# Two loads of attention input ahead of the last two quarters of a weight matrix: the order of transfers in a fused attention and expert kernel

## The chip, the cores and the metric

The kernel runs on one core of a Trainium2 chip. A core has five engines with their own instruction queues: PE (TensorE, matrix multiply), DVE (VectorE), ACT (ScalarE), POOL (GpSimd) and SP (SyncE, which here only issues DMAs). The metric is the device time of one execution in microseconds (us); a comparison uses the median of several.

## What is computed

Two stages follow each other. The first is causal linear attention with decay over 4 sequences of 768 positions with 8 heads of 64, in f32. The second takes the attention output as 3072 tokens of 512 values and applies a gated layer with `w_in` (512 x 2048) and `w_out` (2048 x 512).

```python
for b in range(nb):                      # blocks of 64 positions
    intra = einsum('bhic,bhjc->bhij', qb, kb) * Dmask
    intra = einsum('bhij,bhjd->bhid', intra, vb)
    inter = einsum('bhid,bhde->bhie', qb * lam_pow, kv_state)
    out[:, :, sl] = intra + inter
    kv_state = lam_block * kv_state + einsum('bhsd,bhse->bhde', kb * rev_pow, vb)
x = out.transpose(0, 2, 1, 3).reshape(3072, 512)
h = x @ w_in
result = (h * cos(h)) @ w_out
```

## The kernel before, in words

**Tiles.** The 3072 tokens are 24 blocks of 128 tokens, numbered n = 0 to 23. The second stage takes them in nine tiles of 4, 2, 2, 2, 2, 2, 2, 4 and 4 blocks (TILES). Blocks 0 to 3, tile 0, come from two "spans", the first 256 positions of two sequences, and have code of their own (add_span, L579). From block 4 on, blocks go in "ordinary pairs": pair 2 is blocks 4 and 5, pair 3 is blocks 6 and 7, and so on.

**What a tile does.** For each of 16 slices f of the hidden width, four matmuls make a slice of h in PSUM (ps_h, L732), ACT takes the cosine (L738), DVE multiplies (g, L744). Then each block is projected with w_out: 16 matmuls of 512 columns, in four groups of four (ps_f, L778), so that each group needs one quarter of w_out. ACT copies the result (L792), and SP stores it.

**What an ordinary pair does.** Loads of q, k and v (f32, 256 KB each, L253 through add_load, L275), a product or a cast to bf16 for each of the six (prepare, L315: q at L329, k at L333, v at L337), transposes of q and k (for pair 2 on PE, L359, with copies by DVE at L362; from pair 3 on by DMA, L365), scores (ps_s, L407) and masks (DVE, L412), values (ps_o, L470), the update of the carried state (ps_kv, L419), and the carried part (L502). For pair 2 the first q and the second v are prepared by DVE, the second q and the first v by POOL, and both k by ACT.

**The order of the work.** A planner (L57) holds a task list with a duration, an engine, dependencies and a due time for each task. It plays the list through and gives each engine a fixed order of instructions; nothing is reordered later. A DMA is two tasks: the issue on SP or POOL, and a transfer on one shared "DMA" engine. So a changed duration or dependency of one transfer can move any instruction of the program, on any engine.

**The order of the loads.** ORDER (L36) lists the first loads by name: q, k and v of the two spans (q0 to v1), the six pieces of w_in (i0 to i5), the four quarters of w_out (o0 to o3), and the first ordinary loads (q4, q5, k4, k5). After the list come v4 and v5 and all later pairs. The pieces of both weight matrices are cast to bf16 on the way and are issued by POOL (add_w, L294); a quarter of w_out is 512 KB in bf16. All other loads named here are issued by SP. The loop at L817 to L832 turns the list into tasks, and adds a few waits between SP's and POOL's queues by hand:

- q4 waits for nothing by its place, but `pace` (L755, L851, and the manual dependency at L284) makes it wait for DVE's product g of slice 13 of tile 0.
- o3 waits for the landing of q4 (L825).
- v4 waits for the landing of k4 (L823).

`start` (L252) turns such a wait into a semaphore wait of the issuing instruction, so that everything behind it on that queue waits too.

In the order that the planner gives to PE, tile 0's slices of h are followed by its 64 projection matmuls, among which lie the transposes, scores and values of pair 2. Fifty-six of the 64 stand ahead of pair 2's values (L470), and the first that needs o2 is the thirteenth at the earliest.

Of the kernel before, what the change touches and what calls it, by code (L numbers as in the profile page):

```python
# [18 lines left out]
SPANS = 2  # L19
# [6 lines left out]
LOAD_US = 1.22  # L26
# [6 lines left out]
OUTS = [{"qT": ("ACT", "ACT"), "kT": ("ACT", "ACT")}, {"qT": ("ACT", "ACT"), "kT": ("ACT", "ACT")}]  # L33
VALUES_OUT = [("ACT", "ACT"), ("DVE", "ACT")]
STATE_OUT = [("ACT", "ACT"), ("ACT", "ACT")]
ORDER = "q0 k0 q1 k1 v0 v1 i0 i1 i2 i3 i4 i5 o0 o1 o2 q4 q5 k4 k5 o3"  # L36

W_IN = [2, 2, 1, 3, 4, 4]

# [105 lines left out]
def kernel(  # L145
# [23 lines left out]
    def where(n):  # L169

        if n < 2 * SPANS:
            return n // 2, n % 2
        g, c = divmod(n // 2, NB)
        return 2 * g + n % 2, c
# [4 lines left out]
    loads = ctx.enter_context(tc.tile_pool(name="loads", bufs=BUFS["ld"]))  # L179
# [61 lines left out]
    load_t, issue_t = {}, {}  # L241
    last_issue = {}

    def dma(queue, us, issue_us, emit, prio, deps=(), get=None, ordered=True, lat=1.9):
        t = pl.add(queue, issue_us, list(deps) + [last_issue.get(queue) if ordered else None], emit, prio, get=get)
        if ordered:
            last_issue[queue] = t
        d = pl.add("DMA", us, [t], None, prio, lat=lat)
        d.issue = t
        return t, d  # L250

    def start(queue, o, x, deps):  # L252
        i = queue.dma_start(out=o, in_=x)  # L253
        for d in deps:
            tc.add_manual_dep(i.ins, d.issue.ins.ins.name, mybir.DependencyInfo(
                mybir.DependencyClass.Sync, mybir.DependencyReason.DATA), reason="order of loads")
        return i

    def add_span_load(name, src, x, prio, deps):
        def emit(_):  # L260
            if on_pool:
                t = span_v[x]
            else:
                if ("raw", x) not in live:
                    live["raw", x] = work.tile([P, 2, H, 2, D], F32, tag="g", name="sp_f")
                t = live[name, "sp", x] = live["raw", x][:, "qk".index(name[0])]
            return start(nc.gpsimd if on_pool else nc.sync, t.rearrange("u h s d -> u h (s d)"),
                         src[x, :, 0:2 * P, :].rearrange("h (u s) d -> u h (s d)", s=2), deps)

        on_pool = name == "v_f"  # L270
        issue, load_t[name, "sp", x] = dma("POOL" if on_pool else "SP", 1.5, 1.0 if on_pool else 0.5, emit, prio, deps,
                                           lat=0.95 if on_pool else 1.0)
        return load_t[name, "sp", x]

    def add_load(n, name, src, prio, deps=()):  # L275
        b, c = where(n)

        def emit(_):
            t = loads.tile([P, H, D], F32, tag=name, name=name)
            live[name, n] = t  # L280
            i = start(nc.sync, t, src[b, :, c * P:(c + 1) * P, :].transpose([1, 0, 2]), deps)
            if (name, n) == ("q_f", 2 * SPANS):

                tc.add_manual_dep(i.ins, pace[0].ins.ins.name, mybir.DependencyInfo(  # L284
                    mybir.DependencyClass.Sync, mybir.DependencyReason.DATA), reason="order of loads")
            return i

        issue_t[name, n], load_t[name, n] = dma("SP", LOAD_US, 0.85, emit, prio, deps, get=name,
                                                lat=1.9 if name == "v_f" and n < 2 * SPANS + 2 else 1.0)
        return load_t[name, n]  # L290

    w_t, pace = {}, []

    def add_w(which, c, prio, deps=()):  # L294
        def emit(_):
            if which == "in":
                a, z = sum(W_IN[:c]) * P, sum(W_IN[:c + 1]) * P
                return start(nc.gpsimd, w_in_sb[:, :, a:z], w_in_src[:, :, a:z], deps)
            a, z = c * KF // WCH, (c + 1) * KF // WCH
            return start(nc.gpsimd, w_out_sb[:, a:z, :], w_out_src[:, a:z, :], deps)  # L300

        part = W_IN[c] / 4 if which == "in" else 1.0
        early = which == "in" and c < 3
        _, w_t[which, c] = dma("POOL", 2.68 * part, 0.8, emit, -2000.0 if early else prio, deps,
                               lat=1.2)
        return w_t[which, c]
# [503 lines left out]

    names = ORDER.split()
    for pr in range(SPANS, NBLK // 2):
# [4 lines left out]
    for at, name in enumerate(names):  # L817
        which, n = name[0], int(name[1:])
        soft = which in "io"
        deps = [kept[-3 if soft else -2]] if at and (names[at - 1][0] in "io") != soft else []  # L820
        if name == f"q{2 * SPANS}":
            deps = []
        if name == f"v{2 * SPANS}":  # L823
            deps = [load_t["k_f", 2 * SPANS]]
        if name == "o3":  # L825
            deps = [load_t["q_f", 2 * SPANS]]
        if soft:
            kept.append(add_w({"i": "in", "o": "out"}[which], n, at, [] if at < 9 else deps))
        elif n < SPANS and at < 9:
            kept.append(add_span_load(which + "_f", src[which], n, at - 2040, kept[0:1] if name == "v0" else []))  # L830
        else:
            kept.append(add_load(n, which + "_f", src[which], at, deps))  # L832
# [15 lines left out]
        add_ffn(i)  # L848
    for f in range(3, SPLIT):
        hid[2 * f].deps.append(spans[1]["carried"])  # L850
    issue_t["q_f", 2 * SPANS].deps += pace  # L851
    closing.deps.append(v12[SPANS])
    first_sum.deps += Vo[2 * SPANS]
    lead_end = hid[2 * SPLIT]
# [76 lines left out]
```

## Time and profile before

| what | us |
|---|---|
| median of 3 runs | 202.83 (202.78 to 202.98) |
| profiled execution, its time | 202.54 |
| profiled execution, its span | 200.8 |
| PE busy in the span | 195.9 |
| DVE, ACT, POOL busy | 116.3, 119.4, 64.9 |
| first projection of tile 0 on PE, by the chain | 28.99 |
| SP's first q_f issue of pair 2 | 28.74 |
| POOL's issues of w_out, first three and last | 14.45 to 16.7, and 32.55 |

The span is the profile's own time from the first to the last instruction; the time of an execution also has what lies around it. The page of the profile gives busy time by engine, a view of the span in 40 slices, the DMA queues, and the chain of work that ended last: followed back from the last instruction, at each step to what released it. A row of the timeline gives start, length, engine, line and operation, and in brackets the idle time ahead of it and what ended that. An "x2" means that two instructions are merged in a row. A DMA's row is its issue only; its time to landing is asked for apart.

### The profile page before, as it was taken

What the parts mean: (1) busy time and instruction counts of PE and PEld (TensorE: products, weight loads), DVE (VectorE), ACT (ScalarE), POOL (GpSimd) and SP (SyncE); (2) the same over time, 40 slices, a digit from 0 to 9 for tenths busy, and PEclk for the clock granted to TensorE, in tenths of its full rate; (3) what the DMA queues carried; (4) which work ended last, traced back from release to release, by engine and by line L of the source; (5) the groups of instructions that cost most, each with busy time, mean ns of one, the idle gap of its engine ahead of it and who ended that gap; (6) DMA issues with size and microseconds to landing.
All of it is one profiled execution on the core that took longest, in us unless ns stands there. A gap on an engine that the chain in (4) does not pass through costs nothing.

```text
span 200.8 us, 5951 instructions
## 1 busy us (share of the span) xinstructions
PE 195.9 (98%) x2473; PEld 116.8 (58%) x2473; DVE 116.3 (58%) x230; ACT 119.4 (59%) x241; POOL 64.9 (32%) x85
## 2 busy tenths in 40 slices
PE   6999999999999999999999999999999999999994
PEld 3477444558757757766658676755445544444452
DVE  3978771269756948758458575835588354444001
ACT  4878771149658768666639666644887564345120
POOL 5893003085235360635555353545500000000000
PEclk9999999999999999999999999999999999999999
DMA  5999999999889997999999899979910010111112
GB/s 163 303 190 204 203 199 216 209 238 225 200 197 225 262 202 177 239 179 253 189 275 245 188 207 194 277 141 261 243 23 3 3 52 0 52 55 52 52 52 104
DMA packets 96620, 33.93 MB, mean 169 GB/s; under 512 B 84690, under 2 KB 93650, under 8 KB 96594
## 3 DMA queue, kind: packets, MB, share of 16 engines
q1 hardware_dynamic: 89088, 28.78, 63.2%
q0 software_dynamic: 7360, 4.72, 16.4%
q8 instruction: 19, 0.31, 0.7%
q10 hardware_dynamic: 146, 0.07, 0.1%
q14 instruction: 7, 0.06, 0.1%
HBM read 27.26 MB, written 6.29 MB: 167 GB/s over the span
## 4 chain that ended last, share of the span: by engine, by line
PE 95%; DMA 2%; ACT 0%; DVE 0%; SPq 0%; issue 0%; ACTq 0%; DVEq 0%
PE ps_h L732 42%; PE ps_f L778 42%; DMA sp_f<-in_k_dram 2%; PE ps_s L407 2%; PE ps_o L502 2%; PE ps_o L470 2%; PE ps_kv L419 1%; PE ps_t L601 1%; PE ps_s L612 1%; PE ps_o L638 1%; PE ps_kv L625 1%; PE ps_x L470 0%; PE ps_idle L870 0%; PE ps_t L359 0%; DVE k_sp L593 0%; PE ps_o L644 0%
## 5 line engine op out<-in xcount | busy, mean ns | idle before, releaser
L744 DVE TENSOR_TENSOR g<-ps_h,cos 128x256 bf16<-128x256 f32 (+1 forms) x149 | 73.1, 501 | 42.0 <-ACT cos L738 41.1
L738 ACT ACTIVATE cos<-ps_h,halfpi 128x256 f32<-128x256 f32 (+1 forms) x149 | 75.9, 536 | 29.3 <-PE ps_h L732 28.2
L778 PE MATMUL ps_f<-w_out_sb,g 128*128 128x512 bf16 (+2 forms) x400 | 91.4, 371 | 0.0
L732 PE MATMUL ps_h<-xT,w_in_sb 128*128 128x256 bf16 (+1 forms) x596 | 91.1, 303 | 0.0
L732 PEld LDWEIGHTS <-w_in_sb 128*128 128x128 bf16 x596 | 57.5, 98 | 30.1 <-DVE xT L510 0.4
L778 PEld LDWEIGHTS <-g 128*128 128x128 bf16 x400 | 37.6, 98 | 37.2
L329 POOL TENSOR_TENSOR qk<-q_f,q_scale 128x512 bf16<-128x512 f32 x19 | 20.0, 1067 | 34.7 <-DMA q_f<-in_q_dram 17.6
L792 ACT COPY o_sb<-ps_f 128x512 f32<-128x512 f32 (+1 forms) x24 | 13.7, 572 | 24.7 <-PE ps_f L778 24.5
L337 POOL TENSOR_TENSOR v_s<-v_f,v_scale 128x512 bf16<-128x512 f32 x19 | 19.6, 1042 | 9.8 <-DMA v_f<-in_v_dram 5.2
L412 DVE TENSOR_TENSOR s_m<-ps_s,mask 128x512 bf16<-128x512 f32 x20 | 13.0, 685 | 4.2 <-PE ps_s L407 3.6
L333 POOL CAST qk<-k_f 128x512 bf16<-128x512 f32 x18 | 11.0, 611 | 10.4 <-DMA k_f<-in_k_dram 10.2
L510 ACT CAST xT<-ps_o 128x512 bf16<-128x512 f32 x11 | 6.0, 588 | 9.0 <-PE ps_o L502 5.6
L425 DVE TENSOR_TENSOR sum<-sum,ps_kv 128x512 f32<-128x512 f32 x15 | 10.2, 682 | 0.6
L430 ACT CAST S<-sum 128x512 bf16<-128x512 f32 x15 | 9.1, 616 | 0.9 <-DVE sum L425 0.8
L253 POOL DMA_DIRECT2D w_out_sb<-in_moe_w_out_dram x4 | 3.0, 784 | 15.8 <-DMA q_f<-in_q_dram 15.8
L792 DVE COPY o_sb<-ps_f 128x384 f32<-128x384 f32 x1 | 0.6, 557 | 11.6 <-DMA out_dram<-o_sb 11.6
L470 PEld LDWEIGHTS <-v_s 64*64 64x64 bf16 x320 | 4.0, 107 | 4.2 <-issue 3.4
L870 PE MATMUL ps_idle<-blank 128*128 128x512 f32 (+2 forms) x8 | 4.7, 707 | 1.7 <-DVE blank L215 1.7
L487 DVE COPY spare<-ps_o 1x1 f32<-1x1 f32 x6 | 0.9, 156 | 8.4 <-PE ps_o L470 8.4
L617 DVE TENSOR_TENSOR s_m_sp<-ps_s,mask_sp 128x512 bf16<-128x512 f32 x8 | 5.1, 684 | 1.2 <-PE ps_s L612 1.2
L470 PE MATMUL ps_o<-s_m,v_s 64*64 64x64 bf16 x256 | 5.2, 196 | 0.0
L502 PE MATMUL ps_o<-qkT,S 64*64 64x64 bf16 x304 | 4.9, 195 | 0.0
(76 smaller groups left out, 90.1 us busy)
## 6 DMA issues: line engine op xcount, KB each, us to landing
q_f<-in_q_dram SPq DMA_DIRECT2D x20, 256.0 KB, 3.9
k_f<-in_k_dram SPq DMA_DIRECT2D x20, 256.0 KB, 4.2
v_f<-in_v_dram SPq DMA_DIRECT2D x20, 256.0 KB, 5.1
out_dram<-o_sb SPq DMA_DIRECT2D x19, 256.0 KB, 2.5
w_out_sb<-in_moe_w_out_dram POOLq DMA_DIRECT2D x4, 512.0 KB, 12.4
sp_f<-in_q_dram SPq DMA_DIRECT2D x2, 512.0 KB, 4.9
sp_f<-in_k_dram SPq DMA_DIRECT2D x2, 512.0 KB, 5.5
w_in_sb<-in_moe_w_in_dram POOLq DMA_DIRECT2D x2, 512.0 KB, 8.9
```

Source lines behind the costliest of these rows:

```text
L329: vec[e].tensor_mul(new_qk()[:, 0, :, s], live.pop(("q_f", 2 * pr + s)), q_scale[:, c, :].unsqueeze(2).to_broadcast([P, H, D]))
L333: (nc.scalar.copy if early else nc.gpsimd.tensor_copy)(new_qk()[:, 1, :, s], live.pop(("k_f", 2 * pr + s)))
L337: vec[e].tensor_mul(live["v_s", 2 * pr + s], live.pop(("v_f", 2 * pr + s)), v_scale[:, c, :].unsqueeze(2).to_broadcast([P, H, D]))
L412: nc.vector.tensor_mul(t, live["s", pr][s], mask.unsqueeze(1).to_broadcast([P, H, D]))
L425: nc.vector.tensor_add(new, live["sum", pr, 0] if half else live["sum", pr - 1, 1], live["kv", pr][half])
L430: nc.scalar.copy(new_S(pr, half), live["sum", pr, half])
L470: yield lambda h=h: nc.tensor.matmul(o[halves[h % 2], h // 2], lhsT=live["v_s", n0 + s][m, h, :], rhs=live["s_m", n0 + s][m, h, :], start= ...
L732: nc.tensor.matmul(t[:, :n], lhsT=w_in_sb[:, kd, f * P:(f + 1) * P], rhs=live["xT", i][:, kd, at], start=(kd == 0), stop=(kd == KD - 1))
L738: nc.scalar.activation(c[:, :n], live["h", i, f, at.start][:, :n], AF.Sin, bias=halfpi)
L744: return nc.vector.tensor_mul(live["g", i][:, f, at], live.pop(("h", i, f, at.start))[:, :n], live.pop(("c", i, f, at.start))[:, :n])
L778: nc.tensor.matmul(live["f", i, j, piece][:, :width], lhsT=live["g", i][:, f, j * P:(j + 1) * P], rhs=w_out_sb[:, f, part], start=(f == 0) ...
L792: (nc.scalar.copy if eng == "ACT" else nc.vector.tensor_copy)(o[:, :width], live["f", i, j, piece][:, :width])
```

## The change

In ORDER, q4, q5, k4 and k5 move ahead of o2. The waits change with it: q4 waits for the landing of o0 in place of the product of slice 13 (`pace` is no longer used); o2, in place of o3, waits for the landing of q4; v4 waits for the landing of o2 in place of k4. The planner is told other durations: 0.95 in place of 1.22 for the transfers of pair 2, and a latency of 1.0 in place of 1.9 for that pair's v.

```diff
-ORDER = "q0 k0 q1 k1 v0 v1 i0 i1 i2 i3 i4 i5 o0 o1 o2 q4 q5 k4 k5 o3"
+ORDER = "q0 k0 q1 k1 v0 v1 i0 i1 i2 i3 i4 i5 o0 o1 q4 q5 k4 k5 o2 o3"
...
             i = start(nc.sync, t, src[b, :, c * P:(c + 1) * P, :].transpose([1, 0, 2]), deps)
-            if (name, n) == ("q_f", 2 * SPANS):
-
-                tc.add_manual_dep(i.ins, pace[0].ins.ins.name, mybir.DependencyInfo(
-                    mybir.DependencyClass.Sync, mybir.DependencyReason.DATA), reason="order of loads")
             return i
 
-        issue_t[name, n], load_t[name, n] = dma("SP", LOAD_US, 0.85, emit, prio, deps, get=name,
-                                                lat=1.9 if name == "v_f" and n < 2 * SPANS + 2 else 1.0)
+        issue_t[name, n], load_t[name, n] = dma("SP", 0.95 if n < 2 * SPANS + 2 else LOAD_US, 0.85, emit, prio, deps, get=name,
+                                                lat=1.0)
...
         if name == f"q{2 * SPANS}":
-            deps = []
+            deps = [w_t["out", 0]]
         if name == f"v{2 * SPANS}":
-            deps = [load_t["k_f", 2 * SPANS]]
-        if name == "o3":
+            deps = [w_t["out", 2]]
+        if name == "o2":
             deps = [load_t["q_f", 2 * SPANS]]
...
-    issue_t["q_f", 2 * SPANS].deps += pace
```

Through the planner the change also moves instructions that it doesn't name. On PE, 12 of tile 0's projections move from ahead of pair 2's values (L470) to behind them, pair 3's scores come earlier among the matmuls of tiles 0 and 1, and later tiles are interleaved differently. On SP, pair 3's two transposing DMAs move in between the first stores instead of standing behind all four of them. On DVE, pair 2's product of q moves ahead of the last product of tile 0. The instructions of POOL stand in the same order as before; only what they wait for is changed.

## The prediction

> **What bounds the kernel now.** I read the page's busy shares and its chain first, to see which engine owns the time; then the chain of waits between 27 and 46 us, where the moved transfers are used; then the timelines of SP, POOL and DVE there, for the issues; then each DMA's time from issue to landing, asked for one instruction at a time.
>
> The page, busy time and chain by engine:
>
> ```profile
> PE 195.9 (98%) x2473; PEld 116.8 (58%) x2473; DVE 116.3 (58%) x230; ACT 119.4 (59%) x241; POOL 64.9 (32%) x85
> PE 95%; DMA 2%; ACT 0%; DVE 0%; SPq 0%; issue 0%; ACTq 0%; DVEq 0%
> ```
>
> TensorE bounds it. A busy PE can hide stalls, so I checked the pace in the chain of waits (start, length, what):
>
> ```profile
> 28.99 6.04 PE ps_f L778 x28
> 35.03 0.45 PE ps_t L359 x8
> 35.48 1.73 PE ps_f L778 x8
> 37.20 0.45 PE ps_t L359 x8
> 37.65 1.73 PE ps_f L778 x8
> 39.38 0.62 PE ps_kv L697 x32
> 40.00 0.38 PE ps_s L407 x32
> 40.38 2.69 PE ps_f L778 x12
> 43.07 0.25 PE ps_o L470 x16
> ```
>
> 28 matmuls in 6.04 us and 8 in 1.73 are both 0.216 us each, the pace that also holds at the end (80 in 13.87 = 0.173 with its narrower pieces). A group of four that follows 64-row work takes 0.97 instead of 0.86. From 14 us to 197.9 us every row stands at such a pace: PE never waits there. So **a reordering of transfers has next to nothing to win**; it can only lose, if PE is made to wait.
>
> Now the issues, SP's timeline and then POOL's and DVE's (start, length, instruction):
>
> ```profile
> 28.74 0.99 SPq L253 DMA_DIRECT2D q_f<-in_q_dram  x2
> 29.77 2.13 SPq L253 DMA_DIRECT2D k_f<-in_k_dram  x2
> 33.89 0.99 SPq L253 DMA_DIRECT2D v_f<-in_v_dram  x2
> 34.93 5.05 SPq L253 DMA_DIRECT2D q_f<-in_q_dram  x2
> ```
>
> ```profile
> 14.45 2.27 POOL L253 DMA_DIRECT2D w_out_sb<-in_moe_w_out_dram  x3
> 32.55 0.74 POOL L253 DMA_DIRECT2D w_out_sb<-in_moe_w_out_dram  x1 [15.83 <-DMA q_f<-in_q_dram]
> 33.31 1.06 POOL L329 TENSOR_TENSOR qk<-q_f,q_scale 128x512 bf16<-128x512 f32 x1
> ```
>
> ```profile
> 41.71 1.15 DVE L337 TENSOR_TENSOR v_s<-v_f,v_scale 128x512 bf16<-128x512 f32 x1
> ```
>
> I call the four quarters of w_out o0 to o3, the first ordinary pair's loads q4 q5 k4 k5 v4 v5. By issue plus time to landing, o0 landed at 25.97, o1 at 28.52, o2 at 31.12 (2.55 to 2.6 apart), q4 at 32.02, q5 at 32.92, k4 at 33.81; k5 by 35.6, where ACT's cast of it starts; o3, 6.6 after its issue, at 39.14; v4 at 40.08, v5 at 40.97. The DMA share stays at or above 1 in every 2 us from 28 to 40: these transfers queue on each other.
>
> **The skill against the trace.** "DMA: Bandwidth & Descriptors", Issuing engines are not separate DMA queues, says that transfers issued by different engines run on the same 16 DMA engines and interleave. The first half fits. The second does not carry here: q4 landed 3.3 us after its issue, v4, issued 1.34 us after o3, took 6.2 and landed 0.94 after o3; and SP's next q_f issues were held for 5.05 us. v waited for o3 to finish. I forecast by order of issue, not by shares. Its section Anatomy of one DMA fits a POOL-issued DMA as 2.0 us + bytes/436e3; for a quarter (128x4x512 f32 read, 1 MiB) that is an estimate of 4.4 us. The trace has 6.6 for o3, issued while k5 was still under way. I take 6.6; 4.4 is the other bound.
>
> **The change, part by part.**
>
> *No work is added or removed.* PE has the same matmuls, and as many returns from 64-row to 128-row work (16 before and after, 0.11 us each), so its work costs the same. POOL and SP issue the same DMAs. The new planner durations are no instructions; they only change the order.
>
> *q4's wait.* SP now waits for the landing of o0 (25.97) in place of a gate product (28.7). q4, q5, k4, k5 issue from 26.0, while o1 is under way, as they were before while o2 was. The place of the pattern is one quarter earlier: in before, q4 landed 0.90 after the quarter in flight. So q4 lands at 28.52+0.90 = 29.4, q5 30.3, k4 31.2, k5 about 33.0. o1 is first needed at 28.99+4x0.216 = 29.85; 1.3 us of slack hides any push from the new neighbours.
>
> *o2 behind q4.* POOL used to wait here with o3 only. It resumed 0.53 after q4's landing (32.02 to 32.55), so o2 issues at 29.95, o3 at 30.7. Behind them on POOL stands q5's product: 31.45 to 32.5. PE wants the pair's first transposes after 16 projections, 28.99+16x0.216 = 32.44: some 0.15 us late, swallowed by the next wait. o2 lands at 29.95+6.6 = 36.55, o3 2.6 later at 39.15. PE first wants o2 after 28 projections and two sets of transposes: 28.99+6.04+0.90 = 35.93. **A new wait of 0.6 us.** (In before o2 was there at 31.12, ahead of its use.) k5's cast, 33.0+0.62, is ahead of the second transposes at 34.62.
>
> *v behind o2.* SP issues v4 at 36.6 instead of 33.89. Is it late by that? In both kernels the same six transfers (q4 q5 k4 k5 and two quarters) follow in one queue before v, and start from the same point, one load shorter or longer. So o3 ends at 39.1 in both, and v4 lands 0.94 behind it: 40.1; by its own issue, 36.6+3.3 = 39.9, which is earlier. v5: 41.0, as before. Behind v on SP stand q and k of the next pair; they were held up to 39.07 and 39.98 anyway.
>
> *What is late next.* v's time does not move, but PE's need for it does. Before its first value matmuls PE now has 44 projections of tile 0 instead of 56, since 12 were moved behind. It arrives at 43.07-12x0.216 = **40.48**. The values need v5's product on DVE: 40.97 + 0.05 + 0.69 (such a product without POOL beside it: q4's took 0.69) to 1.15 (the row above, POOL beside it), and about 0.1 to PE. POOL's v4 product now runs 40.2 to 41.25, so little of it lies beside: I take 0.75, and get **41.9**. In before DVE began this product only at 41.71, behind the masks, and was done at 42.86 under PE's projections; that cover is gone.
>
> *Sum.* The waits are not added: the earlier ones delay PE towards the same last deadline. Total 41.9-40.48 = 1.4 us. After it PE has no idle time in which to earn it back. The next pair's scores have 12 projections and 4 tile-1 matmuls of 0.109 fewer ahead of them than before: 54.80-3.0+1.4 = 53.2. They need transposes whose landing was 52.31 (49.57 + 2.74) and which now stand between the stores instead of behind all of them; of the cover of 2.5 us, 0.9 is left. The pair after it had 2.0 us (66.17 for 68.13) and is reached 0.8 earlier (4 projections and 12 such matmuls fewer, 2.2, against 1.4 of wait). Both cost nothing.
>
> Profiled execution: span 200.8, its run 202.54 (1.74 outside), the median 202.83. 200.8+1.4 = 202.2 of span; median 202.83+1.4 = **204.2**.
>
> Bounds of the new waits: at least 0 (o2 after 4.4 us, below); at most 1.4 + 0.4 (DVE at 1.15) + 0.5 (o2 and v half a microsecond later) = 2.3. A gain is excluded but for about 0.1 us, as PE waits nowhere in the stretch.
>
> **Rivals.**
>
> 1. *Not slower: the quarter is quick.* o3's 6.6 us was in part k5's tail (ACT's cast waited to 35.6). If POOL's transfers start at once, o2 takes 4.4: 29.95+4.4 = 34.35, before 35.93; o3 36.9; v4 the later of 34.4+3.3 and 36.9+0.94, 37.85; v5 38.75; product done 39.6, before 40.48. No wait: 202.8. It decides when v5 lands before 39.6. For it: 2.55 between quarters in a filled queue. Against: k5 is again in front, and the DMA share leaves little room to finish six transfers 2.2 us sooner.
> 2. *Slower still.* q and k, now beside o1, and two quarters close together push o2's landing by 1 us (time to landing of the POOL issues ranges up to 15.2 when queued). SP then issues v4 at 37.6, v5 lands at 42.0, and PE waits 2.4: 205.2. For it: v's chain has no slack left. Against: the bytes ahead are the same.
> 3. *Faster.* Only if the new interleaving shortened PE's own rows, for which no row speaks: 202.3.
> 4. *The change does nothing*, as SP or POOL are busy elsewhere: excluded. SP had waited 23.9 us ahead of q4 and POOL 15.8 ahead of o3.
>
> **Numbers.** Forecast 204.2 (own range 203.5 to 204.9): 0.66. Rival 1: 0.15. Rival 2: 0.13. Rival 3: 0.06. The range reaches down to rival 1 and up to rival 2's centre: 202.7 to 205.3. Within 0.2% (0.4 us, about what a measurement of this kernel can tell from no change) is rival 1, 0.15; faster 0.06; slower the rest, 0.79.
>
> **What would show it.** Right: SP's first q_f issue near 26.0; POOL's third quarter near 29.95, landing near 36.5; PE idle ahead of a ps_f L778 group near 36 (DMA w_out_sb) and ahead of the ps_o values near 40.5 to 41.9 (DVE v_s, itself waiting for v_f); v5 landing near 41.0; every later row shifted by the same amount. Wrong: o2 landing before 35.9 and v5 before 39.6 (rival 1); q4 landing later than 30, which would say that o1 and the loads do share; waits of PE past 50 us, which I costed at nothing.

## The result and the profile after

The changed kernel takes 205.38 us (median of 6 runs, 204.88 to 206.28) against 202.75 us for the kernel before on the same chip (6 runs, 202.61 to 202.98): a ratio of 1.0132, with a 95% interval of 1.0109 to 1.0154. The loss is 2.6 us where the forecast had 1.4. The time lies above the forecast's own range (203.5 to 204.9) and just above the wider one, which ended at rival 2's centre (205.3). The profiled execution took 205.60 us, 3.06 more than the profiled one before (202.54).

The page of the changed kernel, busy time and chain by engine:

```profile
PE 196.4 (96%) x2473; PEld 116.8 (57%) x2473; DVE 115.5 (57%) x230; ACT 119.2 (58%) x241; POOL 64.6 (32%) x85
PE 77%; DMA 16%; POOL 2%; SPq 1%; issue 1%; DVE 0%; ACT 0%; POOLq 0%; ACTq 0%
```

PE does the same 2473 matmuls in nearly the same busy time (196.4 against 195.9). What changed is the chain: PE's share fell from 95% to 77%, and 16% now lies with transfers (their length on the chain, not idle time of PE), so somewhere PE waited for one. PE's timeline of the changed kernel gives the place (start, length, engine, line, operation; in brackets the idle time ahead of the row and what ended it):

```profile
28.95 3.62 PE L774 MATMUL ps_f<-w_out_sb,g 128*128 128x512 bf16 x16
32.72 0.62 PE L355 MATMUL ps_t<-ident,qk 128*128 128x128 bf16 x8
33.17 1.89 PE L774 MATMUL ps_f<-w_out_sb,g 128*128 128x512 bf16 x8
34.90 0.61 PE L355 MATMUL ps_t<-ident,qk 128*128 128x128 bf16 x8
35.35 1.03 PE L774 MATMUL ps_f<-w_out_sb,g 128*128 128x512 bf16 x4
37.60 1.02 PE L774 MATMUL ps_f<-w_out_sb,g 128*128 128x512 bf16 x4 [1.23 <-DMA w_out_sb<-in_moe_w_out_dram]
...
43.55 0.32 PE L466 MATMUL ps_o<-s_m,v_s 64*64 64x64 bf16 x16 [1.23 <-DVE v_s L333]
```

Two waits of 1.23 us: one for o2, one for the product of v5, both where the forecast had put them. (The line numbers are 4 lower than before: four lines of code are gone.) The first transposes are 0.28 later than the 32.44 worked out from the kernel before: 0.13 because PE began its projections that much later in this execution (28.95 against 28.82), and 0.15 of wait behind the last projection (32.57), as forecast. The values begin at 43.55. Without waits they would have begun at 40.48, so PE has lost 3.07 us by then: that 0.13, the three waits of 0.15, 1.23 and 1.23, and some 0.3 for starting again after the first two (the four projections behind the wait for o2 took 1.02, and 0.86 at the pace of before). The last long row of the chain, 80 projections, starts at 187.16 in the changed kernel and at 184.07 before: 3.09 later. All of the difference but 0.13 is made between 29 and 44 us, none after it. The trace names no wait of PE past 50 us.

The chain of waits of the changed kernel from 26 us on (start, length, what) says what the values waited for:

```profile
26.13 3.45 DMA q_f<-in_q_dram
...
30.11 7.45 DMA w_out_sb<-in_moe_w_out_dram
37.56 0.02 issue
37.58 0.37 SPq L253
...
37.99 4.79 DMA v_f<-in_v_dram
42.78 0.02 issue
42.81 0.70 DVE v_s L333
43.51 0.04 issue
43.55 0.32 PE ps_o L466 x16
```

q4 lands, POOL resumes 0.5 us later and issues o2 at 30.11; o2 takes 7.45 us; SP, which sat on v4 for that, issues v4 and v5 within 0.4 us; v5 takes 4.79 us; DVE's product takes 0.69; PE goes on. Every link but two is as forecast: the two transfers were longer.

SP's timeline of the changed kernel shows the gap between k and v, which no other load fills:

```profile
27.16 2.29 SPq L253 DMA_DIRECT2D k_f<-in_k_dram  x2
37.58 0.99 SPq L253 DMA_DIRECT2D v_f<-in_v_dram  x2
```

The table by stretches of the changed kernel (stretch, its length, busy us and count of PE, PEld, DVE, ACT and POOL, then granted clock, DMA share, GB/s) shows what that does to the transfers:

```profile
32.00:34.00 2.00, 1.85 (x15) 0.93 (x14) 0.62 (x1) 0.88 (x2) 0.66 (x1) 1.00 0.85 124
36.00:38.00 2.00, 0.77 (x4) 0.29 (x3) 0.24 (x1) 0.00 (x0) 0.00 (x0) 1.00 1.19 198
38.00:40.00 2.00, 2.00 (x69) 1.23 (x68) 0.25 (x1) 0.59 (x1) 0.06 (x1) 1.00 0.76 160
```

In the kernel before, the first and the last of these stretches were:

```profile
32.00:34.00 2.00, 2.00 (x11) 0.88 (x9) 0.69 (x1) 0.16 (x1) 1.44 (x2) 1.00 1.07 243
38.00:40.00 2.00, 2.00 (x47) 1.06 (x49) 0.38 (x1) 0.00 (x0) 0.00 (x0) 1.00 1.15 259
```

The DMA share falls to 0.85, from 1.07, while o2 starts up behind the last of k, and to 0.76, from 1.15, while v4 starts up behind o3; in slices of half a microsecond it falls to 0.3 at 32.0 and to 0.4 at 38.0. The queue runs nearly dry twice, where the forecast had six transfers without a gap.

Does that set v's landing? A transfer is done when the last of 16 DMA engines has reported its part, and the trace has the time of each report. I took the median and the last report of each transfer from it:

| transfer | before: median, last | changed: median, last |
|---|---|---|
| k5 | 34.60, 35.58 | 32.19, 32.70 |
| o2 | 30.19, 31.12 | 35.74, 37.56 |
| o3 | 38.24, 39.14 | 38.31, 40.11 |
| v4 | 39.14, 40.08 | 40.35, 41.05 |
| v5 | 40.06, 40.97 | 41.31, 42.78 |

The median engine was through with o2 at 35.74, before PE wanted it (36.37 in this trace), and with o3 at 38.31, as early as before. The last engine trails it by 1.8 us for o2 and o3, where the last one trailed by 0.9 for o3 before. It is the last one that PE, SP and DVE wait for. The dry spell moved v4's median by 1.2, but v4's landing stands 0.94 behind o3's, the same as before and as forecast. So v4 was late because o3's last engine was (its own late issue would give the same landing here; experiment 8 parts the two), and v5 then fell another 0.84 behind.

### The profile page after: what moved, and what is told of

Same layout as the page of the kernel before. It is cut to its first block, busy times and chain, and to the rows that moved or that the text cites. A ratio compares the mean times of both kernels' runs of the same rounds, so it can differ in the third digit from the quotient of the medians.

```text
span 203.9 us, 5950 instructions
## 1 busy us (share of the span) xinstructions
PE 196.4 (96%) x2473; PEld 116.8 (57%) x2473; DVE 115.5 (57%) x230; ACT 119.2 (58%) x241; POOL 64.6 (32%) x85
## 4 chain that ended last, share of the span: by engine, by line
PE 77%; DMA 16%; POOL 2%; SPq 1%; issue 1%; DVE 0%; ACT 0%; POOLq 0%; ACTq 0%
PE ps_f L774 36%; PE ps_h L728 34%; DMA w_out_sb<-in_moe_w_out_dram 9%; DMA sp_f<-in_k_dram 3%; DMA v_f<-in_v_dram 2%; DMA q_f<-in_q_dram 2%; PE ps_o L498 2%; PE ps_o L466 2%; POOL w_in_sb L253 1%; PE ps_kv L415 1%; PE ps_s L403 1%; SPq L253 1%; POOL k_sp L589 1%; PE ps_x L466 0%; DVE v_s L333 0%
## 5 line engine op out<-in xcount | busy, mean ns | idle before, releaser
L774 PE MATMUL ps_f<-w_out_sb,g 128*128 128x512 bf16 (+2 forms) x400 | 93.1, 371 | 1.2 <-DMA w_out_sb<-in_moe_w_out_dram 1.2
L728 PE MATMUL ps_h<-xT,w_in_sb 128*128 128x256 bf16 (+1 forms) x596 | 92.6, 303 | 0.0
L421 DVE TENSOR_TENSOR sum<-sum,ps_kv 128x512 f32<-128x512 f32 x15 | 10.2, 683 | 0.8
L253 POOL DMA_DIRECT2D w_in_sb<-in_moe_w_in_dram x6 | 4.6, 777 | 0.0
```

The costliest lines, as they stand in the source:

```text
L421: nc.vector.tensor_add(new, live["sum", pr, 0] if half else live["sum", pr - 1, 1], live["kv", pr][half])
L728: nc.tensor.matmul(t[:, :n], lhsT=w_in_sb[:, kd, f * P:(f + 1) * P], rhs=live["xT", i][:, kd, at], start=(kd == 0), stop=(kd == KD - 1))
L774: nc.tensor.matmul(live["f", i, j, piece][:, :width], lhsT=live["g", i][:, f, j * P:(j + 1) * P], rhs=w_out_sb[:, f, part], start=(f == 0) ...
```

## The experiments

The theory after the result, A in the texts below: PE reaches the values 2.6 us earlier than before, since 12 projections were taken from ahead of them, and what is lost is set by the last of v5's chain (q4, o2, v4, v5, product) against that arrival. Other letters are the rivals of the run concerned, and are told in its expectation. The kernel before was run beside each batch: 202.71 to 202.72. The ratios are to those runs. "Waits" are those of PE between 28 and 46 us in the profiled execution.

For the experiments that change what a load waits for, and not the order of instructions, the wait lists are kept and replaced after the planner has given its order:

```diff
+        given[name] = deps        # in the loop over ORDER, ahead of "if soft:"
...
     tc.plan = plan
+    given["..."][:] = [...]       # one line or more for each experiment
```

### 1. v5's landing taken away

```diff
-            vec[e].tensor_mul(live["v_s", 2 * pr + s], live.pop(("v_f", 2 * pr + s)),
+            vec[e].tensor_mul(live["v_s", 2 * pr + s], live.pop(("k_f" if pr == SPANS else "v_f", 2 * pr + s)),
```

(The k tile is kept alive for it by `live.get` in `prep_k`.)

> The changed kernel, in which the v products of pair 2 read k4 and k5 in place of v4 and v5 (so its attention values of that pair are other numbers); v4 and v5 are still loaded. It takes away PE's wait for v and nothing else. Theory A (the last deadline, v, sets the whole loss of 2.6 us; the waits in front of it are swallowed): what is left is the wait ahead of the transposes (0.25) and that for o2 (1.2 to 1.4), about 1.5 in all: 204.2. Rival B (the loss lies in the new order on PE or in later stretches): 205.4, as the changed kernel.

Measured: 203.97 (203.19 to 205.44, 8 runs), ratio 1.0061 [1.0035, 1.0087]. PE's timeline of this kernel:

```profile
32.74 0.62 PE L355 MATMUL ps_t<-ident,qk 128*128 128x128 bf16 x8 [0.17 <-POOL qk L325]
37.01 1.02 PE L774 MATMUL ps_f<-w_out_sb,g 128*128 128x512 bf16 x4 [0.62 <-DMA w_out_sb<-in_moe_w_out_dram]
41.66 0.32 PE L466 MATMUL ps_o<-s_m,v_s 64*64 64x64 bf16 x16
```

The wait at the values is gone, the one for o2 stays (0.62 in this execution). 1.4 of the 2.6 us went with v's landing; the other 1.25 are there with v out of play. The profiled execution, at 205.44, is the slowest of the eight and has a further wait past this stretch, for the transposing DMA of a later pair; its rows above are read for the places only.

### 2. o2's landing taken away

```diff
-                                             rhs=w_out_sb[:, f, part], start=(f == 0), stop=(f == KF - 1))
+                                             rhs=w_out_sb[:, f % 8 if i == 0 else f, part], start=(f == 0), stop=(f == KF - 1))
```

> The changed kernel, in which tile 0's projections of slices 8 to 15 read the first two quarters of w_out in place of o2 and o3 (so tile 0's output is another). It takes away PE's wait for o2; SP still issues v4 at o2's landing. Theory A (last deadline): PE arrives earlier at the values and waits there the whole 3 us; 205.4, unchanged. Rival C (each wait costs for itself, the sum counts): 1.2 to 1.4 less, 204.1.

Measured: 205.05 (204.84 to 205.16, 6 runs), ratio 1.0107 [1.0087, 1.0127]. Waits: 0.29 at the first transposes, none for o2, and at the values 1.72 (1.23 in the changed kernel):

```profile
42.77 0.32 PE L466 MATMUL ps_o<-s_m,v_s 64*64 64x64 bf16 x16 [1.72 <-DVE v_s L333]
```

Taking 1.2 us of wait away gained 0.33: PE only reached the values earlier and waited there. The two waits do not add; the last deadline sets the loss, as A has it.

### 3. The cover put back by the planner

The planner is told later landings for o2 and o3 and for v, so that it orders PE otherwise; transfers and waits are those of the changed kernel.

```diff
-                               lat=1.2)
+                               lat={2: 3.4, 3: 3.4}.get(c, 1.2) if which == "out" else 1.2)
...
-                                                lat=1.0)
+                                                lat=1.8 if name == "v_f" and n < 2 * SPANS + 2 else 1.0)
```

> The changed kernel with the same transfers and waits, but the planner is told a later landing of o2 and o3 (latency 3.4 in place of 1.2) and of v4 and v5 (1.8 in place of 1.0). PE's order then has 32 projections ahead of the first that needs o2 and 56 ahead of the values, as before the change. Theory A: PE needs o2 at 37.8 (landing 37.6) and v5 at 43.2 (ready 43.5): waits of 0.3 to 0.6 in all, 203.2 (202.8 to 203.7). Rival B: the late transfers cost wherever PE's projections stand, 205.4.

Measured: 203.09 (202.69 to 203.86, 14 runs), ratio 1.0012 [0.9999, 1.0025]. PE's timeline:

```profile
35.25 1.89 PE L774 MATMUL ps_f<-w_out_sb,g 128*128 128x512 bf16 x8
37.07 0.69 PE L693 MATMUL ps_kv<-v_sp,k_sp 128*64 128x64 bf16 x32
37.70 0.45 PE L403 MATMUL ps_s<-qkT 64*64 64x64 bf16 x32
38.08 5.35 PE L774 MATMUL ps_f<-w_out_sb,g 128*128 128x512 bf16 x23
43.60 0.32 PE L466 MATMUL ps_o<-s_m,v_s 64*64 64x64 bf16 x16 [0.17 <-DVE v_s L333]
```

Eight projections, not four, now stand behind the second transposes, and the first that needs o2 starts only at 38.08; then 24 of them (the trace has records of 23) instead of 12 lie ahead of the values. The transfers are no quicker: o2 takes 7.04 us and v5 lands at 42.72, as late as in the changed kernel (42.78). Yet 2.2 of the 2.6 us are back. The late landings cost next to nothing where PE has other work in front. (The planner's new answer also differs from the changed kernel's order past 56 us. PE waits for no transfer there in either, and the changed kernel's shift stayed at 3.1 us from 44 to 187 us, so what came back lies ahead of the values.) This is the strongest evidence for A: PE's order, not the transfers by themselves, turned the landing times into loss.

### 4. v not held back by o2

Edit to the changed kernel: `given["v4"][:] = [load_t["k_f", 4]]`, as in the kernel before. The order stays.

> The changed kernel with all orders kept; v4 waits for k4's landing (as before the change) in place of o2's, so it issues near 31.7 in place of 37.6. Theory A1 (transfers of SP and POOL are served in the order of issue: o2 and o3, issued 30.1 and 30.8, go first): v4 lands 0.9 behind o3, at 41.0, as in the changed kernel; 205.2 to 205.5. Theory A2 (served by who is ready, and POOL's start slowly): v and what stands behind it on SP go ahead of o2, o2 lands 2 to 7 us later, PE waits for o2 instead: 206 to 211. Rival D (SP's wait for o2 is the whole cause, v would land at 35): 204.2, only the o2 wait left.

Measured: 205.35 (204.58 to 205.58, 4 runs), ratio 1.0127 [1.0097, 1.0156]. SP's timeline:

```profile
31.44 1.00 SPq L253 DMA_DIRECT2D v_f<-in_v_dram  x2
32.48 8.13 SPq L253 DMA_DIRECT2D q_f<-in_q_dram  x2
```

v4 was issued 6.1 us earlier than in the changed kernel and landed at 40.67, 9.23 us later, behind o3 (40.14); v5 landed at 41.56. SP's next loads were held for 8.13 us. So the queue did not run dry here (DMA share 1.23 from 38 to 40), and v still came behind POOL's two quarters. By the sizes of the packets in the trace, SP's loads (v4, v5 and q of the next pair) moved 8 KB from 33 to 36 us, beside 523 of POOL's quarters, and 87 KB from 36 to 38.5, beside 373: next to nothing at first and a fifth later. In this profiled execution, the quickest of the four, v5 was 1.2 us earlier than in the changed kernel, 0.4 of it by v4. The medians are equal (205.35 and 205.38), so no part of the 1.2 us by which the forecast fell short is shown to lie with v's gate or the dry spell behind it.

### 5. New order, old waits

Edits to the changed kernel's wait lists: q4 waits for o1's landing, o2 for nothing, o3 for q4, v4 for k4. POOL and SP then issue at about the times of the kernel before, while PE keeps the order of the changed kernel.

> The changed kernel with every engine's order kept, but the waits of before: q4 waits for o1's landing (28.6, as the gate product did at 28.7), o2 is issued at once, o3 waits for q4, v4 for k4. It shows what the new order of PE, DVE and SP costs with the old transfers. Theory A (PE waits where its order outruns a landing): q5 lands 32.9, its product is done on POOL at 34.4, so PE waits about 2.0 ahead of the first transposes; after that v5, ready near 42, is early for 42.5: 204.7 to 204.9. Rival B (the new transfers are the fault, the order is harmless): 202.7. Rival E (v alone): 204.1.

Measured: 205.84 (204.89 to 206.56, 6 runs), ratio 1.0154 [1.0122, 1.0186], 1 us above what A gave. PE's timeline:

```profile
34.55 0.62 PE L355 MATMUL ps_t<-ident,qk 128*128 128x128 bf16 x8 [1.98 <-POOL qk L325]
...
43.10 0.32 PE L466 MATMUL ps_o<-s_m,v_s 64*64 64x64 bf16 x16 [0.33 <-DVE v_s L333]
```

The old waits don't bring the old time back under the new order: PE now comes to the first transposes 2 us before POOL has q5's product. The values, at 43.10, are 0.45 earlier than in the changed kernel, and this execution took 205.17. The six runs fall into two groups: three of 204.89 to 205.17, at a mean granted clock of 1.00, and three of 206.51 to 206.56, at 0.992. The excess over A's number is the second group; experiment 11 takes it up.

### 6. Old order, early q and k

The kernel before with its q4 waiting for o0's landing: the dependency on `pace` is left out and `given["q4"][:] = [w_t["out", 0]]`.

> The kernel before with every engine's order kept; only q4's wait is changed, from the gate product (28.7) to o0's landing (26.0), so that SP's four loads stand beside o1 and o2 in the DMA engines for 2.7 us longer. Theory A1 (served in the order of issue): q4 still lands at about 32 behind o2 and nothing moves: 202.7. Theory A2 (the queues interleave): q4 lands before 30.5, o2 later than 31.6 where PE wants it: 203.5 to 205.

Measured: 202.79 (202.56 to 203.14, 14 runs), ratio 1.0001 [0.9993, 1.0009]. q4 was issued at 26.07 instead of 28.74 and landed at 32.24, against 32.02 before: it stood behind o2 (31.49) for 6.18 us. With o2 issued ahead, an earlier issue of q and k moved no landing. Only taking o2 out of their way does (29.58 in the changed kernel), and o2 pays for it.

### 7. o2 issued a little earlier

Edit to the changed kernel: o2 waits for o1's landing in place of q4's.

> The changed kernel; o2 waits for o1's landing (28.65) in place of q4's (29.6), so POOL issues it near 29.2 in place of 30.1. If o2's landing goes by its issue (7.1 later on the mean of the traces so far): lands 36.3, v4 and v5 as much earlier, 204.4 to 204.7. If it goes by the end of k5 in front of it in the engines: lands near 37.2 as before, 205.1 to 205.4.

Measured: 209.27 (208.6 to 209.93, 4 runs), ratio 1.0321 [1.0297, 1.0346]: 4 us more than expected, the largest miss of the study. PE's timeline:

```profile
39.55 1.03 PE L355 MATMUL ps_t<-ident,qk 128*128 128x128 bf16 x8 [4.90 <-ACT qk L329]
40.37 3.62 PE L774 MATMUL ps_f<-w_out_sb,g 128*128 128x512 bf16 x8
```

o2 was issued at 28.98, 1.1 us earlier, and landed later, at 37.89 (8.91 us). k5, issued 0.28 us before o2, landed behind it, at 38.85, after 10.15 us; ACT's cast and PE's second transposes waited for k5. That is 4.90 us of wait in place of none. Then eight projections took 3.62 us, 0.45 each instead of 0.216. The table by stretches of this kernel:

```profile
36.00:38.00 2.00, 0.00 (x0) 0.00 (x0) 0.00 (x0) 0.00 (x0) 0.00 (x0) 0.84 1.12 184
38.00:40.00 2.00, 0.45 (x5) 0.46 (x6) 0.00 (x0) 0.62 (x1) 0.00 (x0) 0.50 0.67 138
40.00:42.00 2.00, 2.00 (x10) 0.96 (x8) 0.69 (x1) 0.00 (x0) 0.00 (x0) 0.50 0.95 214
42.00:44.00 2.00, 2.00 (x9) 0.52 (x9) 0.00 (x0) 0.00 (x0) 0.00 (x0) 0.50 1.00 226
```

The granted clock (third from the end) fell to 0.50 during the wait and stayed there until 44 us. The wait cost once as idle time and once more in the slow matmuls behind it. The Trainium skill, "TensorE: Matmul & The Clock Gate", Part 1: The HAM clock gate, says that PE's clock halves after an idle window of about 3.4 us and comes back after as long a busy one. The halving and the return fit it (PE resumed at 39.55, the clock was back at 44.2), the 3.4 us of idle time do not: PE stopped at 34.65 and the clock fell at 37.4, 2.7 us later, and in experiment 9 it fell 2.3 us after PE had stopped. The expectation had left the clock out.

### 8. o3 issued later

Edit to the changed kernel: o3 waits for k5's landing, so that o2 is issued alone.

> The changed kernel; o3 waits for k5's landing (32.7)[...]. q5's product stands behind it on POOL, so PE waits 2.7 in place of 0.25 ahead of the first transposes, and the time is 205.3 to 205.8 in any case. What it tells is o2's time to landing: 6.6, as o3 alone had before the change, if two quarters issued together are what made it 6.8 to 7.5; unchanged, if not.

Measured: 206.8 (205.15 to 207.04, 4 runs), ratio 1.0182 [1.0151, 1.0214]. o2 took 6.46 us, o3 7.45. v4, issued at 36.63, landed at 41.36: 4.73 us after its issue (3.47 in the changed kernel) but 0.89 behind o3 (0.94), so it is o3's end and not its own issue that v4 went by. There is no wait for o2 and none at the values, but one of 2.46 at the first transposes: q5's product stands behind o3's issue on POOL, and o3 waited. The profiled execution, at a clock of 1.00, took 205.15; the other three had 0.992 and took 206.60 to 207.04. One quarter alone was not clearly quicker than two (below), and a wait taken from one instruction of POOL was given to the next in its line.

### 9. Old order, new waits

The kernel before with the waits of the changed one; o2's issue is moved behind q4's so that it can wait for q4.

> The order of PE, DVE, ACT and SP of before, with the transfers and waits of the changed kernel (q4 behind o0, o2 and o3 behind q4, v4 behind o2). The fourth corner of the square of orders and waits. Theory A: PE wants o2 after 12 projections, at 31.6, and gets it at 36.6 to 37.6: a wait of 5 to 6 us; v is then no longer late. If the half clock after a long wait comes too, as in the run where PE waited 4.9 us and lost 6.5, it is 209 to 211; without it 208 to 208.8. Rival F (the new order on PE is what costs, the waits do not): 202.7.

Measured: 210.1 (210.07 to 210.65, 4 runs), ratio 1.0349 [1.0287, 1.0411], as expected. PE's timeline:

```profile
37.12 5.40 PE L774 MATMUL ps_f<-w_out_sb,g 128*128 128x512 bf16 x16 [5.49 <-DMA w_out_sb<-in_moe_w_out_dram]
```

The old order asks for o2 as early as 31.6 us, so it waits 5.49, and 16 matmuls behind the wait take 0.34 each at a clock of 0.50 to 0.81. With experiments 5, 6 and 3 this closes a square:

| us | old waits | new waits |
|---|---|---|
| old order on PE | 202.7 | 210.1 |
| new order on PE | 205.8 | 205.4 |
| order planned with late landings | not run | 203.1 |

Neither half of the change is the cause by itself: the new waits under the old order are far worse than both together, and the new order under the old waits is no better than both (205.8, with half of its executions at the lower clock). What is common to the lossy cells is a deadline of PE that comes before its landing.

### 10. Cover and v set free together

Experiment 3 with the edit of experiment 4.

> The changed kernel with the later landings told to the planner (56 projections ahead of the values, as in e3) and with v4 waiting for k4 in place of o2 (as in e4). v5 then lands near 41.6 in place of 42.7, and its product is ready at 42.4, before PE's 43.2; o2 at 37 is before 37.8. Theory A: no wait is left, 202.6 to 202.9, the time of before. It cannot be below 202.6, as PE's work is the same. If some cost of the new transfers is left that the waits don't show: 203.0 to 203.5.

Measured: 203.11 (202.91 to 203.46, 14 runs) against 202.72, ratio 1.0003 [0.9979, 1.0027]. v5 landed at 40.85 and the wait at the values is gone. One wait is left in the stretch:

```profile
32.72 0.62 PE L355 MATMUL ps_t<-ident,qk 128*128 128x128 bf16 x8 [0.30 <-POOL qk L325]
```

It is q5's product behind the issues of o2 and o3 on POOL, the wait that the forecast put at 0.15, seen by itself. By medians the version is 0.4 slower than the kernel before, which the interval doesn't separate from none. No version run here beats the kernel before, whose PE had no wait to give up.

### 11. Old waits, PE kept busy

Experiment 5 with six matmuls of ident by ident ahead of the first transposes, so that most of the 2 us of idle time is filled.

```diff
+            if pr == SPANS and i == 0:
+                f = bank(t.bank[0], [P, 4 * P], F32, "ps_idle")
+                for _ in range(6):
+                    nc.tensor.matmul(f, lhsT=ident, rhs=ident.unsqueeze(1).to_broadcast([P, 4, P]), start=True, stop=True)
```

> The kernel of e5 (new order, old waits), with six matmuls of 128x512 (1.3 us, their result is not used) on PE ahead of the first transposes, in the middle of its wait of 2.0 us there. e5 ran at 204.9 to 205.2 with a mean clock of 1.00 in some executions and at 206.5 with 0.992 in others. If the lower clock comes of PE's idle time: all executions at 204.8 to 205.3 with a clock of 1.00. If it has nothing to do with the wait: the same two groups, 204.9 and 206.5. If a longer wait has another cause: times over 205.5 at a clock of 1.00.

Measured: 205.01 (204.55 to 205.47, 9 runs), ratio 1.0098 [1.0068, 1.0128]. The first transposes start at 34.65, no earlier than in experiment 5 (34.55), but all nine executions have a clock of 1.00 and there is no group at 206.5. None of nine against three of six: this points to PE's idle time, through the clock, as the origin of the second group of experiment 5, 1.5 us slower. The size agrees: a mean of 0.992 over 204.8 us is, by estimate, 3.3 us at 0.50. The traces of its slower executions were not taken, so where in them the clock fell is not shown.

### 12. The changed kernel again

> The changed kernel once more, for the scatter of its landings in a second trace. In the first, o2 took 7.45 us and v5 landed 1.73 behind v4. If o2's 7.45 is at the upper end of a scatter (6.8 to 7.3 in the experiments), and v5's extra 0.8 comes and goes: the time lies at 204.9 to 205.4 and the trace shows v5 near 42 and PE's waits summing to 2.2 to 3.0. If they are a fixed cost: 7.4 and 42.8 again.

Measured: 205.58 (204.48 to 207.34, 6 runs), ratio 1.0127 [1.0074, 1.018]; the run of 207.34 had a clock of 0.992. The profiled execution took 206.22. In its timelines of PE and DVE:

```profile
37.40 1.02 PE L774 MATMUL ps_f<-w_out_sb,g 128*128 128x512 bf16 x4 [1.14 <-DMA w_out_sb<-in_moe_w_out_dram]
44.05 0.32 PE L466 MATMUL ps_o<-s_m,v_s 64*64 64x64 bf16 x16 [1.94 <-DVE v_s L333]
```

```profile
43.31 0.69 DVE L333 TENSOR_TENSOR v_s<-v_f,v_scale 128x512 bf16<-128x512 f32 x1 [2.47 <-DMA v_f<-in_v_dram]
```

o2 took 7.37 us, as in the first profile (7.45), and v4 again 3.5. v5 landed 2.42 behind v4, where it had been 1.73 in the first profile and 0.9 before the change. o2's length came again; v5's lag scatters, and its 0.7 more is the 0.6 by which this execution is slower.

## Why the prediction missed: step by step

The direction, the places of both waits and what each waits for were right. What failed is the size of two terms of the sum, the 6.6 us for o2's landing and the 0.9 from v4 to v5. The sum was 1.65 short: it had the values ready at 41.9, and they began at 43.55.

- **No work added; nothing lost or earned back later.** Right: the same busy time, the same shift of 3.1 us at 44 and at 187 us.
- **q4's wait.** Right: q4 issued at 26.13 and landed at 29.58 (29.4 forecast), q5 30.49, k4 31.63, k5 32.70 (33.0). o1 landed at 28.65, ahead of its use at 29.8.
- **"o2 issues at 29.95, o3 at 30.7."** Right: 30.11 and 30.84, and a wait of 0.15 at the first transposes.
- **"o2 lands at 29.95+6.6 = 36.55."** The step that failed: a term of the sum that was mis-sized. It landed at 37.56, 0.16 by its issue and 0.85 by its length of 7.45. The 6.6 was one transfer in one execution, and it is two things: the median engine's time, which is steady (5.7 for o3 before; 5.4 to 5.6 in the profiles of the changed kernel and experiments 1, 2, 3 and 10; but 6.7 in experiment 7, where o2 was issued 1.1 us earlier), and the lag of the last engine behind it, which is not (0.9 before; 1.8, 1.9, 1.9, 1.5, 1.5 and 0.6 in the changed kernel, its second profile and experiments 2, 1, 3 and 10). With o2 and o3 issued together, o2 took 5.96 to 7.45 in eight profiles (7.45, 7.37, 7.33, 7.04, 7.01, 6.84, 6.81, 5.96; mean 7.0; with the 8.91 of experiment 7, 7.2). A quarter issued alone took 5.87 to 7.92 (o3: 6.59, 7.92, 7.80, 5.87; o2 in experiment 8: 6.46; mean 6.9; o3 there, issued apart but close behind o2, 7.45). The prediction's other bound, 4.4, was reached by none. So "two together are slower" is not shown, and what makes the last engine late in a quarter is open. One sample of a scattered term had been taken as its value.
- **"v's time does not move."** Failed as a consequence. It rested on o3's end at 39.1 in both kernels, plus 0.94. The 0.94 came exactly, and o3's median engine ended as early as before (38.31 and 38.24), so the argument of the same six transfers held for that. But o3's last engine ended at 40.11, in line with o2's (2.55 behind it in the last, 2.57 in the median): v4 at 41.05 for 40.1. In 11 of the 14 profiles (before, changed and twelve experiments) v4 landed 0.8 to 0.9 behind o3.
- **v5 0.9 behind v4.** Failed by 0.8: it was 1.73, and 2.42 in experiment 12. The cause is open. v5's last engine came 1.5 to 2.5 behind the median in seven of the 14 profiles, and in each an instruction-fetch transfer of 16 KB, about 1 us long, had started while v5 was under way. But five others, the kernel before and experiments 2, 4, 6 and 10, had one as well, with lags of 0.4 to 1.0, and o2's last engine was 1.8 behind in the changed kernel with no such transfer in its time. It was not tested by moving the fetch.
- **The product: 0.75 to DVE.** Right: 0.69 and some hundredths each side.
- **"The waits are not added."** Right, by experiment 2: 1.2 us of wait removed gained 0.33.
- **12 projections taken from ahead of the values as the cost.** Right, by experiment 3: giving them back returned 2.2 of 2.6 us with the transfers as late as ever.
- **The rivals.** Rival 2 (v5 at 42.0, 205.2 us) came nearest. It had o2's landing 1 us late, as it came. Its ground, that q and k beside o1 and two quarters close together push o2, is not shown (o1 landed on time, and see the times of a quarter above), so the number came without the reason. I had given it 0.13, with "the bytes ahead are the same" against it: that argues for the median engine, and PE waits for the last one.

The Trainium skill, "DMA: Bandwidth & Descriptors", Issuing engines are not separate DMA queues, has transfers interleave whoever issues them, and the forecast went by order of issue instead. Experiment 4 shows both in part. SP's loads did move beside the quarters, but with 8 KB to 523 at first and a fifth of the bytes later, and v4 and v5 landed behind them. Experiment 7 shows that order of issue is no rule either: k5, issued ahead of o2, landed behind it.

## What to carry to other kernels

A wait put on a landing ties everything behind it to the slowest of 16 DMA engines, whose lag scattered here by a microsecond or more and mostly passed from o2 to o3 (1.8 and 1.8, 1.9 and 1.7, 0.6 and 0.7 in the changed kernel and experiments 2 and 10); take such a term from many transfers, as a range, and not from one. Ask of a reordering what it takes from ahead of each deadline: the same late transfers cost 2.6 us with 44 matmuls in front and 0.4 with 56 (not clearly apart from none). In an engine that never waits, earlier transfers buy nothing; what sets the time is how much work is left to cover the latest one, and a planner's landing times must be those of the trace, or a little later.

## What the runs showed of the hardware

- The last of 16 DMA engines came 0.5 to 2.4 us behind the median one in a quarter of w_out (0.46 in experiment 6, 2.42 in experiment 5), in kernels that issue the same transfers.
- A quarter of w_out under way from POOL's queue left SP's loads 8 KB to its 523 and later a fifth of the bytes (experiment 4). A load issued long before the quarter ended took 6.2 (q4, experiment 6), 9.2 (v4, experiment 4) or 10.2 us (k5, experiment 7); issued some 2.5 us before the quarter's landing, 3.3 to 3.5 (q4 before, q4 and v4 in the changed kernel).
- In idle times of PE of 4.9 and 5.5 us the granted clock fell to 0.50, 2.7 and 2.3 us after PE had stopped, and stayed there for 6.8 us (experiments 7 and 9). With a profiled wait of only 2.0 to 2.5 us, three of six and three of four executions of experiments 5 and 8 had a mean clock of 0.992 and took some 1.5 us more; with most of that wait filled, none of nine had (experiment 11).
